# Background transform of k·v: spectra stored from the background's clock, the next channel tile begun at once, transposes seven or nine ticks behind the product

## The chip, the cores and the metric

The kernel runs on one core of one Trainium2 chip. The metric is the device time of one execution in microseconds, less is better. A time given for a kernel is the median of its runs; the profile comes from one more execution, which is read on its own time.

## The reference

Two rounds of a long-convolution layer and a feed-forward layer, each with a residual and a layer norm, on 2048 tokens of 1024 channels, in fp32:

```python
def _A_ref(q, k, v, shift_k, ssm_k, ssm_D):
    ...
    kv = k_shift * v                     # k_shift: causal depthwise conv over 4 tokens
    ...
    y_f = kv_f * kf_f                    # spectra over 2*S of kv and of ssm_k
    y = irfft(y_f)[:S]                   # so: a causal depthwise conv over all 2048 tokens
    y = y + kv * ssm_D
    return q * y

def _B_ref(x, w1, b1, w2, b2):
    h = relu(x @ w1 + b1) ** 2           # 1024 -> 3584
    return h @ w2 + b2                   # 3584 -> 1024

x = A_q
x = x + _A_ref(_layernorm(x), A_k, A_v, ...)
x = x + _B_ref(_layernorm(x), B_w1, ...)
x = x + _A_ref(_layernorm(x), A_k, A_v, ...)
x = x + _B_ref(_layernorm(x), B_w1, ...)
```

Of the convolution only q depends on the layer before. The convolution of k·v with `ssm_k` depends on the inputs alone, so one result serves both rounds.

## The kernel before

The tokens are cut into four blocks of 512 (`sb` or `b`, 0 to 3), the channels into eight tiles of 128 (`c`). The feed-forward matmuls run in seven **units**, each a layer and a token block, in the order (0,0), (1,0), (0,1), (0,2), (1,1), (0,3), (1,2), the last one together with (1,3). An fp32 product is made of three fp32r matmuls of a high and a low half (`mm3`, lines 353, 354 and 355), so nearly all of TensorE's work carries one of these three lines. A unit is a list of **steps** of twelve such matmuls. The weights for them are loaded (`wr`), cast to the high half on ScalarE (line 1102), and the low half is subtracted on VectorE, sometimes on GpSimd (line 1110). Line 1098 loads halves that an earlier unit stored in `wd_m`; line 1118 stores them. Line 1587 makes the low half of a feed-forward activation.

Beside the steps goes the **background**, which makes the convolution of blocks 1 to 3 while the units run. It consists of generators that are advanced by a *tick* at a time; what they issue in a tick stands between two pieces of the main work.

- `fwd_x` transforms one channel tile of k·v, `fwd_g` one of `ssm_k`. Each has its stream over blocks and channel tiles. `fwd_tick` advances both streams by one yield. It is called 1.4 times per step in the first three units and less often later, not at all in the last steps of most units, and once more wherever the product stream has nothing to do.
- `prod_stream` multiplies the stored spectra on GpSimd (line 543), sums on VectorE (line 547), folds on GpSimd or VectorE (lines 693 to 698), transforms back on TensorE (for block 1 line 613), and evicts on ScalarE (line 619) into a row buffer named `wr`, of the ring that also holds weights as they are loaded.

The background's clock `plag` (a `Later`) counts the ticks of the product stream; `plag.at(n, f, ...)` calls `f` n ticks on. When both streams are through with a tile, its entry in `fwd_done` is set three ticks on, and only then is its spectrum read (line 643).

`fwd_x` for one tile is: load k and v (lines 373 and 375), four ticks, scale on ScalarE (380), three multiply-adds on VectorE for the four-token convolution (383), the product with v (385), then a number of empty ticks (386), then one bank of the PSUM ring `pt` is taken and TensorE transposes the product into it (called in line 389, issued in line 438). ScalarE copies the result out (393), for blocks 2 and 3 split into two halves (397 on ScalarE, 399 on VectorE). Two banks are taken for the transform (409 for block 1, three matmuls each for the others), the butterfly runs on VectorE (420, 421, 425), and three spectra go to `XD` in DRAM (430). `fwd_g` has the same shape, with its own lines: transform (472), and on VectorE 482 to 502, of which 501 and 502 are butterflies on `pt` and on `fk`.

The ring `pt` has two banks, shared by the transposes, both transforms and the inverse. Line 613's matmuls and line 438's use it in turn. An engine executes its instructions in the order in which the program issued them. So a place in the tick order is a place in every engine's queue: what TensorE finds there has to be ready, or all the matmuls behind it stand still.

The lines that the change touches are 386 (the number of empty ticks) and 426 to 431 (the store).

Of the kernel before, what the change touches and what calls it, by code (L numbers as in the profile page):

```python
# [248 lines left out]
def tile_h3_mlp(ctx: ExitStack, tc: tile.TileContext, q, kT, vT, shk, ssmT, ssmD, w1, b1, w2, b2,  # L249
# [28 lines left out]
    def mkfx(shape, dt=F32):  # L278
        return cv.tile(shape, dt, name="fx", bufs=4)
# [68 lines left out]
    def give(*tiles):  # L348
        for o in tiles:
            held[slot.pop(id(o))[0]] = False  # L350

    def mm3(o, lh, ll, rh, rl, start, stop):
        PE.matmul(o, lh, rh, start=start, stop=False)  # L353
        PE.matmul(o, lh, rl, start=False, stop=False)  # L354
        PE.matmul(o, ll, rh, start=False, stop=stop)  # L355

    def hold(n):
        got = take(n)
        while not got:
            yield  # L360
            got = take(n)
        return got

    def dview(t, sb, c):
        return t[2 * c:2 * c + 2, :, BT * sb:BT * sb + BT].rearrange("g p b u -> p g b u")
# [5 lines left out]
    def fwd_x(sb, c):  # L371
        k4 = mkfx([P, T + 3])
        SY.dma_start(k4, kT[c * P:(c + 1) * P, sb * T:sb * T + T + 3])
        v4 = mkfx([P, T])
        SY.dma_start(v4, vT[c * P:(c + 1) * P, sb * T:(sb + 1) * T])
        for _ in range(FWD_WAIT):
            yield
        ks = mkfx([P, T])
        w = shkt[:, c]
        A.activation(ks, k4[:, 3:], AF.Copy, scale=w[:, 0:1])  # L380
        yield
        for s in range(1, 4):
            V.scalar_tensor_tensor(ks, k4[:, 3 - s:T + 3 - s], w[:, s:s + 1], ks, op0=OP.mult, op1=OP.add)
        yield
        V.tensor_mul(ks, ks, v4)
        for _ in range(4 if sb == 1 else 7):
            yield
        o, = yield from hold(1)
        transposes(o, ks)
        yield  # L390
        if sb <= PLAIN:
            xt = mkfx([P, T])
            A.copy(xt, o)
        else:
            hi = mkfx([P, T], F32R)
            lo = mkfx([P, T], F32R)
            A.copy(hi, o)
            yield
            V.tensor_sub(lo, o, hi.bitcast(F32))
        yield  # L400
        give(o)
        yield
        oa = yield from hold(2)
        for e in range(2):
            for r in range(2):
                q_ = slice(e * 256, e * 256 + 256)
                ou = oa[e][:, r * 256:r * 256 + 256]
                if sb <= PLAIN:
                    PE.matmul(ou, plain[0][:, 2 * e + r], xt[:, q_], start=True, stop=True)
                else:  # L410
                    mm3(ou, fh[:, 2 * e + r], fl[:, 2 * e + r], hi[:, q_], lo[:, q_], True, True)
        yield
        odd = mkfx([P, T])
        A.copy(odd, oa[1])
        yield
        xo = cv.tile([P, 2, T], F32, name="fy", bufs=1)
        xv = xo.rearrange("p r (n u c) -> p u (r n) c", u=2, c=CG)
        ev = oa[0].rearrange("p (n c) -> p n c", c=CG)
        ov = odd.rearrange("p (n c) -> p n c", c=CG)
        V.tensor_add(xv[:, 0], ev, ov)  # L420
        V.tensor_sub(xv[:, 1], ev, ov)
        yield
        give(*oa)
        x2 = mkfx([P, T])
        V.tensor_add(x2, xo[:, 0], xo[:, 1])
        yield
        yield
        for i in range(3):
            t = x2 if i == 2 else xo[:, i]
            SY.dma_start(dview(XD[i], sb, c), t.rearrange("p (g b u) -> p g b u", g=2, b=BT))  # L430
        yield

    def transposes(o, ks):
        ov = o.rearrange("p (e g b c) -> p e b g c", e=2, g=2, b=BT)
        kv = ks.rearrange("p (b t e) -> p e b t", b=BT, e=2)
        for e in range(2):
            for b in range(BT):
                PE.transpose(ov[:, e, b], kv[:, e, b], ident)
# [75 lines left out]
    plag, slag = Later(), Later()  # L514
# [3 lines left out]
    def fwd_stream(kind, fwd):  # L518
        for sb in range(1, NB):
            if sb > PLAIN:  # L520
                const_split()
            for c in range(KT):
                yield from fwd(sb, c)
                half_done[kind].add((sb, c))
                if all((sb, c) in d for d in half_done.values()):
                    plag.at(3, fwd_done.add, (sb, c))

    streams = [fwd_stream("x", fwd_x), fwd_stream("g", fwd_g)]

    def fwd_tick():  # L530
# [1613 lines left out]
    for s, (k, u, c, a, i, tts, w) in enumerate(steps):  # L2144
# [38 lines left out]
        if k == "m1":  # L2183
# [9 lines left out]
            for kk in range(4):  # L2193
                t = slice(kk * P, (kk + 1) * P)
# [8 lines left out]
        elif k == "w2":  # L2203
# [7 lines left out]
            for n in range(2):  # L2211
                t = slice(n * P, (n + 1) * P)
# [11 lines left out]
        else:  # L2224
# [5 lines left out]
            for tt in tts:  # L2230
                t = slice(tt * P, (tt + 1) * P)
# [124 lines left out]
```

## Time and profile before

| | before |
|---|---|
| median of 3 runs | 2680.07 us (2679.81 to 2684.74) |
| profiled execution, its own time | 2686.72 us |
| its span | 2684.9 us |
| TensorE (PE) busy | 2623.7 us, 98% of the span |
| VectorE (DVE) busy | 2009.8 us, 75% |
| ScalarE (ACT) busy | 1108.6 us, 41% |
| GpSimd (POOL) busy | 1027.9 us, 38% |
| DMA queue, share of 16 engines | 83.3% |

The span is the time from the first to the last instruction in the trace; 1.8 us of the execution's own time lie around it. The profile names an engine, a line and an operation with the tile written and the tile read (`out<-in`), and where an engine stood idle it names the instruction that released it. PEclk is the granted TensorE clock as a share of full speed: 1.00 is 2.4 GHz, 0.50 is 1.2 GHz.

### The profile page before, as it was taken

The numbers are of one execution on the slowest core, as the hardware profiler recorded it, in microseconds if no ns is written. First come the engines' busy times: TensorE is split into PE (matmuls) and PEld (weight loads), VectorE is DVE, ScalarE is ACT, GpSimd is POOL, SyncE is SP. The second block draws the span as 40 slices with busy tenths as digits, with TensorE's granted clock in tenths as the row PEclk, the third lists the DMA queues.
The fourth block names the chain that finished last, engine by engine and source line by source line (L and its number), as shares of the span: only waits on it lengthen the run. The fifth ranks groups of instructions, "written<-read, shape, count | busy, mean of one in ns | idle before, by whom it ended". The sixth has DMA issues, their size and how long they took to land.

```text
span 2684.9 us, 36134 instructions
## 1 busy us (share of the span) xinstructions
PE 2623.7 (98%) x12388; PEld 2197.9 (82%) x12388; DVE 2009.8 (75%) x2948; ACT 1108.6 (41%) x1891; POOL 1027.9 (38%) x651
## 2 busy tenths in 40 slices
PE   7999999899999999999999999999999999999999
PEld 6888787787888888888888888888788778888887
DVE  7879888789887877779677765456777788877553
ACT  4454344443444333343232422345444565454342
POOL 2436665256551744427554275000100207535111
PEclk9999999999999999999999999999999999999999
DMA  8789898689989999888987888689889787888663
GB/s 254 262 300 313 293 305 280 231 292 357 345 296 315 308 329 304 273 300 303 340 303 255 306 293 306 207 260 321 304 296 304 269 323 251 263 247 317 230 194 121
DMA packets 380264, 763.16 MB, mean 284 GB/s; under 512 B 44064, under 2 KB 159408, under 8 KB 377008
## 3 DMA queue, kind: packets, MB, share of 16 engines
q1 hardware_dynamic: 380080, 760.85, 83.3%
q8 instruction: 98, 1.61, 0.2%
q14 instruction: 86, 0.70, 0.1%
HBM read 583.49 MB, written 177.21 MB: 283 GB/s over the span
## 4 chain that ended last, share of the span: by engine, by line
PE 79%; DVE 8%; DMA 8%; issue 2%; ACT 2%; POOL 2%; SPq 1%; DVEq 0%; ACTq 0%; POOLq 0%
PE p L353 22%; PE p L354 22%; PE p L355 22%; PE pt L354 2%; PE pt L353 2%; PE pt L355 2%; DMA wr<-w 2%; PE p L1184 2%; DMA whl<-wd_m 2%; DMA cg<-gd 1%; DVE whl L1110 1%; POOL cp L543 1%; DVE sm L547 1%; DVE st L714 0%; DMA cx<-xd 0%
## 5 line engine op out<-in xcount | busy, mean ns | idle before, releaser
L543 POOL TENSOR_TENSOR cp<-cx,cg 128x384 f32<-128x384 f32 (+5 forms) x288 | 544.6, 1904 | 567.7 <-DVE sm L547 378.2
L353 PE MATMUL p<-xh,whl 128*128 128x512 f32 (+1 forms) x1504 | 579.1, 385 | 10.6 <-ACT wr L1924 5.7
L355 PE MATMUL p<-xh,whl 128*128 128x512 f32 (+1 forms) x1504 | 574.9, 382 | 3.5 <-DVE whl L1110 3.0
L354 PE MATMUL p<-xl,whl 128*128 128x512 f32 (+1 forms) x1504 | 574.6, 382 | 0.1
L1110 DVE TENSOR_TENSOR whl<-wr,whl 128x512 fp32r<-128x512 f32 x486 | 430.1, 896 | 130.9 <-ACT whl L1102 126.0
L1102 ACT CAST whl<-wr 128x512 fp32r<-128x512 f32 x546 | 332.4, 619 | 468.7 <-PE p L355 291.7
L353 PE MATMUL p<-whl,rh 128*128 128x512 f32 x1204 | 475.9, 395 | 7.1 <-DMA whl<-wd_m 5.7
L354 PE MATMUL p<-whl,rh 128*128 128x512 f32 x1204 | 471.1, 391 | 2.6 <-POOL whl L1110 1.7
L355 PE MATMUL p<-whl,rl 128*128 128x512 f32 x1204 | 470.6, 391 | 0.0
L353 PEld LDWEIGHTS p<-xh,whl 128*128 128x128 f32 x1504 | 284.9, 189 | 66.2 <-ACT wr L1924 6.4
L355 PEld LDWEIGHTS p<-xh,whl 128*128 128x128 f32 x1504 | 284.7, 189 | 59.1 <-DVE whl L1110 3.4
L354 PEld LDWEIGHTS p<-xl,whl 128*128 128x128 f32 x1504 | 284.7, 189 | 52.4 <-DVE xl L1497 0.3
L1587 DVE TENSOR_TENSOR rl<-wr,rh 128x512 fp32r<-128x512 f32 x140 | 141.7, 1012 | 178.7 <-ACT rh L1584 178.6
L353 PEld LDWEIGHTS p<-whl,rh 128*128 128x128 f32 x1204 | 227.3, 189 | 55.9 <-DMA whl<-wd_m 4.8
L1110 POOL TENSOR_TENSOR whl<-wr,whl 128x512 fp32r<-128x512 f32 x60 | 87.5, 1461 | 483.9 <-ACT whl L1102 426.4
L354 PEld LDWEIGHTS p<-whl,rh 128*128 128x128 f32 x1204 | 227.2, 189 | 49.8 <-DVE whl L1110 2.5
L355 PEld LDWEIGHTS p<-whl,rl 128*128 128x128 f32 x1204 | 226.9, 188 | 47.8
L547 DVE TENSOR_REDUCE sm<-cp 128x128 f32<-128x384 f32 (+5 forms) x288 | 249.4, 874 | 10.2 <-POOL cp L543 10.2
L1579 ACT ACTIVATE wr<-p,b1t 128x512 f32<-128x512 f32 x138 | 95.3, 690 | 369.8 <-PE p L355 368.9
L1707 DVE TENSOR_TENSOR acc<-p,acc 128x512 f32<-128x512 f32 x152 | 99.8, 686 | 83.6 <-PE p L355 83.6
L693 POOL TENSOR_TENSOR sm<-sm 128x512 f32<-128x512 f32 x48 | 69.1, 1440 | 136.2 <-DVE sm L547 130.3
L355 PE MATMUL p<-whl,tq 128*128 128x512 f32 x276 | 107.4, 389 | 0.0
(376 smaller groups left out, 4264.0 us busy)
## 6 DMA issues: line engine op xcount, KB each, us to landing
whl<-wd_m SPq DMA_DIRECT2D x318, 512.0 KB, 5.5
wr<-w SPq DMA_DIRECT2D x442, 256.0 KB, 5.5
wd_m<-whl SPq DMA_DIRECT2D x70, 512.0 KB, 6.3
wr<-td SPq DMA_DIRECT2D x112, 256.0 KB, 5.1
cx<-xd SPq DMA_DIRECT2D x48, 512.0 KB, 5.8
cg<-gd SPq DMA_DIRECT2D x48, 512.0 KB, 6.8
tq<-hd SPq DMA_DIRECT2D x24, 1024.0 KB, 7.2
gd<-fg SPq DMA_DIRECT2D x72, 256.0 KB, 6.4
```

The source lines that it names most:

```text
L353: PE.matmul(o, lh, rh, start=start, stop=False)
L354: PE.matmul(o, lh, rl, start=False, stop=False)
L355: PE.matmul(o, ll, rh, start=False, stop=stop)
L543: G.tensor_mul(pr.rearrange("p c i -> p i c"), xt[:, 0:j + 1], gt[:, j::-1])
L547: V.tensor_reduce(sm[:, ty, jj], st["pr"], axis=AX.X, op=OP.add)
L693: E.tensor_add(s[:, 1:3], s[:, 1:3], s[:, 0:1].to_broadcast([P, 2, s.shape[2]]))
L1102: A.copy(t[:, 0], raws[n]["t"])
L1110: ENG[e[n % len(e)]].tensor_sub(t[:, 1], raws[n]["t"], t[:, 0].bitcast(F32))
L1184: PE.matmul(o, lh, r, start=start, stop=stop)
L1579: A.activation(r, st["o"], AF.Relu, bias=b1t[:, st["f"]:st["f"] + 1])
L1587: V.tensor_sub(st["lo"], st["r"]["t"], st["hi"].bitcast(F32))
L1707: V.tensor_add(accs[tt][:, d], o, accs[tt][:, d])
```

## The change

```diff
@@ fwd_x
         V.tensor_mul(ks, ks, v4)
-        for _ in range(4 if sb == 1 else 7):
+        for _ in range(7 if sb == 1 else 9):
             yield
         o, = yield from hold(1)
         transposes(o, ks)
...
         x2 = mkfx([P, T])
         V.tensor_add(x2, xo[:, 0], xo[:, 1])
+        plag.at(2, store_x, sb, c, [xo[:, 0], xo[:, 1], x2])
         yield
-        yield
-        for i in range(3):
-            t = x2 if i == 2 else xo[:, i]
+
+    def store_x(sb, c, ts):
+        for i, t in enumerate(ts):
             SY.dma_start(dview(XD[i], sb, c), t.rearrange("p (g b u) -> p g b u", g=2, b=BT))
-        yield
```

Three things change. Between the product and its transposes there are seven empty ticks in place of four for block 1, and nine in place of seven for blocks 2 and 3. The three stores are issued two ticks of `plag` after the last addition, by the clock and no longer inside the stream. And the stream gives up two of the three yields around the stores, so that the next tile's loads are issued in the tick after the last addition. A tile of block 1 takes one tick more than before (three added, two dropped), a tile of blocks 2 and 3 as many as before.

Three places show how the instructions move. The first is **TensorE** near the middle of the first unit, at the fifth channel tile of block 1 (tiles counted from the first one that goes through `fwd_x`). `p_...` are the main work's PSUM tiles, `whl` the weights, `rh` and `rl` the activations, `ident,fx` the transposes, `sm,yh` the inverse. Before:

```order
 L354 MATMUL p_2898<-whl,rh 128x512
 L355 MATMUL p_2898<-whl,rl 128x512
 L613 MATMUL pt<-sm,yh 128x128 x4
 L438 MATMUL pt<-ident,fx 128x2x64 x4
 L353 MATMUL p_2895<-whl,rh 128x512
 L354 MATMUL p_2895<-whl,rh 128x512
```

and with the change, where `L613 MATMUL pt<-sm,yh 128x128 x8` stands twelve rows above the transposes:

```order
 L354 MATMUL p_2889<-whl,rh 128x512
 L353 MATMUL p_2890<-whl,rh 128x512
 L354 MATMUL p_2890<-whl,rh 128x512
 L355 MATMUL p_2890<-whl,rl 128x512
 L438 MATMUL pt<-ident,fx 128x2x64 x4
 L353 MATMUL p_2887<-whl,rh 128x512
```

The transposes move down: in the built programs 16 main matmuls lie between the tile's product (line 385 on VectorE) and its transposes before, and 44 now. For the nine tiles from the first on the count goes from 76, 24, 24, 28, 16, 44, 28, 16, 44 to 76, 36, 40, 44, 44, 40, 56, 28, 556.

The second place is **VectorE** at the same tile. Before:

```order
 L501 TENSOR_TENSOR fg<-pt,fg 128x2x2x64
 L502 TENSOR_TENSOR fg<-pt,fg 128x2x2x64
 L383 SCALAR_TENSOR_TENSOR fx<-fx,shkt 128x512 x3
 L501 TENSOR_TENSOR fg<-fk 128x2x2x64
 L502 TENSOR_TENSOR fg<-fk 128x2x2x64
 L1110 TENSOR_TENSOR whl<-wr,whl 128x512
 L385 TENSOR_TENSOR fx<-fx 128x512
 L1110 TENSOR_TENSOR whl<-wr,whl 128x512
 L1587 TENSOR_TENSOR rl<-wr,rh 128x512
 L1110 TENSOR_TENSOR whl<-wr,whl 128x512
```

and with the change:

```order
 L383 SCALAR_TENSOR_TENSOR fx<-fx,shkt 128x512 x3
 L501 TENSOR_TENSOR fg<-pt,fg 128x2x2x64
 L502 TENSOR_TENSOR fg<-pt,fg 128x2x2x64
 L1110 TENSOR_TENSOR whl<-wr,whl 128x512
 L385 TENSOR_TENSOR fx<-fx 128x512
 L501 TENSOR_TENSOR fg<-fk 128x2x2x64
 L502 TENSOR_TENSOR fg<-fk 128x2x2x64
 L1110 TENSOR_TENSOR whl<-wr,whl 128x512
 L1587 TENSOR_TENSOR rl<-wr,rh 128x512
 L1110 TENSOR_TENSOR whl<-wr,whl 128x512 x2
```

The product keeps its neighbours; only a pair of `fwd_g`'s butterflies moves from ahead of it to behind it.

The third place is **SyncE's DMA queue** in the first unit, at the first tile that is stored from the background (the change against the kernel before):

```order
-L430 DMA xd_74<-fy 128x2x256
-L430 DMA xd_75<-fy 128x2x256
-L430 DMA xd_76<-fx 128x2x256
 L373 DMA fx<-kT 128x515
 L375 DMA fx<-vT 128x512
 L1092 DMA wr<-w 128x512 x2
-L1118 DMA wd_m_0_0_2_1739<-whl 128x1024
+L1118 DMA wd_m_0_0_2_1736<-whl 128x1024
+L431 DMA xd_74<-fy 128x2x256
+L431 DMA xd_75<-fy 128x2x256
+L431 DMA xd_76<-fx 128x2x256
```

The stores move behind the next tile's loads of k and v and behind three more transfers of weights.

## Rows read from the trace of the kernel before

**Rows 1.** The page: busy time of each engine, and VectorE's share in 40 slices.

```profile
PE 2623.7 (98%) x12388; PEld 2197.9 (82%) x12388; DVE 2009.8 (75%) x2948; ACT 1108.6 (41%) x1891; POOL 1027.9 (38%) x651
...
DVE  7879888789887877779677765456777788877553
```

**Rows 2.** TensorE's waits, whole span: total us, times, longest us.

```profile
PE pt L438 <- DVE fx L385: 7.6, 3, 5.0
...
PE pt L613 <- DVE fg L502: 2.1, 1, 2.1
...
PE pt L354 <- DVE yl L579: 0.7, 1, 0.7
```

**Rows 3.** TensorE's instructions at the fifth tile: start us, us, engine, line.

```profile
294.31 0.39 PE L354 MATMUL p<-whl,rh 128*128 128x512 f32 x1
294.54 0.39 PE L355 MATMUL p<-whl,rl 128*128 128x512 f32 x1
294.77 1.05 PE L613 MATMUL pt<-sm,yh 128*128 128x128 f32 x8
300.78 1.09 PE L438 MATMUL pt<-ident,fx 128*128 128x128 f32 x4 [4.96 <-DVE fx L385]
```

**Rows 4.** TensorE's instructions at the fourth tile, same columns.

```profile
257.72 1.05 PE L613 MATMUL pt<-sm,yh 128*128 128x128 f32 x8
260.94 0.72 PE L438 MATMUL pt<-ident,fx 128*128 128x128 f32 x4 [2.17 <-DVE fx L385]
```

**Rows 5.** Stretches: us, busy us of each engine, PEclk, DMA share, GB/s.

```profile
261.80:265.20 3.40, 3.40 (x10) 2.63 (x9) 3.40 (x7) 3.34 (x7) 0.00 (x0) 0.50 1.02 338
...
299.40:306.20 6.80, 5.42 (x15) 4.47 (x16) 6.49 (x12) 1.49 (x3) 3.31 (x4) 0.50 1.01 303
...
446.10:449.60 3.50, 3.50 (x11) 2.82 (x11) 3.46 (x6) 0.38 (x1) 2.36 (x2) 0.51 0.00 0
...
637.30:640.70 3.40, 3.40 (x9) 2.64 (x8) 3.40 (x6) 0.18 (x1) 0.49 (x1) 0.50 1.04 378
```

**Rows 6.** VectorE's instructions at the fifth tile: start us, us, engine, line.

```profile
291.73 0.42 DVE L501 TENSOR_TENSOR fg<-pt,fg 128x256 f32<-128x256 f32 x1
...
292.39 3.69 DVE L383 SCALAR_TENSOR_TENSOR fx<-fx,shkt 128x512 f32<-128x512 f32 x3
296.00 1.22 DVE L501 TENSOR_TENSOR fg<-fk 128x256 f32<-128x256 f32 x1
297.14 1.49 DVE L502 TENSOR_TENSOR fg<-fk 128x256 f32<-128x256 f32 x1
298.56 1.48 DVE L1110 TENSOR_TENSOR whl<-wr,whl 128x512 fp32r<-128x512 f32 x1
299.95 0.68 DVE L385 TENSOR_TENSOR fx<-fx 128x512 f32<-128x512 f32 x1
...
301.76 0.68 DVE L1110 TENSOR_TENSOR whl<-wr,whl 128x512 fp32r<-128x512 f32 x1
```

**Rows 7.** GpSimd's instructions at the same time.

```profile
295.49 4.00 POOL L543 TENSOR_TENSOR cp<-cx,cg 128x384 f32<-128x384 f32 x3
```

**Rows 8.** VectorE at the fourth tile; the 1.88 us are three instructions.

```profile
260.12 0.68 DVE L385 TENSOR_TENSOR fx<-fx 128x512 f32<-128x512 f32 x1
...
261.93 1.88 DVE L1110 TENSOR_TENSOR whl<-wr,whl 128x512 fp32r<-128x512 f32 x3
```

**Rows 9.** Line 383, all instances: ns min/median/max, first and last start.

```profile
L383 DVE SCALAR_TENSOR_TENSOR fx<-fx,shkt x72: 706/753/2793, 147.3 to 1411.8; 128x512 f32<-128x512 f32 x72
```

**Rows 10.** Line 619, all instances, and what it waited for (us, times).

```profile
L619 ACT ACTIVATE wr<-pt x16: 377/384/389, 228.7 to 574.1; 128x256 f32<-128x256 f32 x16
...
  DVE whl L1110: 12.1, 4
```

**Rows 11.** SyncE's queue: what the spectrum stores waited for.

```profile
SPq L430 <- DVE fx L425: 12.4, 10, 3.5
```

**Rows 12.** TensorE's waits from 500 to 650 us, columns as in rows 2.

```profile
PE p L353 <- DMA whl<-wd_m: 2.9, 2, 2.1
```

## The prediction

> **What bounds the kernel.** The page comes first: TensorE is busy 98% of the span, VectorE 75%, and in the first third of the span 80 to 90% [rows 1]. A change in the background's order adds no matmul and takes none away, so it can only act on the 2% in which TensorE stands, and on the time that it runs at half clock. Second, the list of TensorE's waits: of those that the edited lines can reach there are three on line 385, 7.6 us together, and one of 2.1 us on line 502 [rows 2]. Third, TensorE's instructions in time: two of the three waits are at the fourth tile, 2.17 us [rows 4], and at the fifth, 4.96 us [rows 3]; the third is what is left of 7.6, 0.5 us. Fourth, the clock: about each long wait there is a stretch with a granted clock of 0.50, and after it the clock is 1.00 again [rows 5]. So a wait costs its idle time and then half of the busy time in its slow stretch.
>
> VectorE tells why TensorE waits at the fifth tile. The product (line 385) is issued 16 matmuls ahead of the transposes, 16 x 0.23 = 3.7 us at the spacing of two starts [rows 3], but VectorE reaches it 8.6 us after that place (3.7 and the 4.96 that TensorE waits): it is late. Its three multiply-adds take 3.69 us where three at the shortest take 2.1 [rows 6, 9], line 501 takes 1.22 us where it took 0.42 a moment before, line 502 takes 1.49 and line 1110 1.48 against 0.68 in the same rows [rows 6]. With 0.42 for line 502 too, the excess is 1.6 + 0.8 + 1.1 + 0.8 = 4.3 us. From 295.49 to 299.49 GpSimd runs three multiplications [rows 7], and from 299.95 VectorE's operations have their short times again.
>
> **The change, part by part.** The sum is made against the profiled execution, 2686.72 us. The median of the runs is 6.65 us lower, and the difference is carried over to it.
>
> *Three more ticks ahead of the transposes, block 1.* The distances count main matmuls between product and transposes.
> - Fourth tile: 28 become 44. TensorE reaches the new place 16 x 0.23 = 3.6 us after the old one, at 258.77 + 3.6 = 262.4; the product was through at 260.8 [rows 8]. The wait goes: 2.17 us, and half of 3.40 busy us at half clock, 1.70 [rows 5]; 3.87 in all. But the transposes now stand directly behind two inverses, and a bank of the ring comes free only when line 619 has evicted it into a row of the weight ring, which waits for line 1110 to have read the row (line 619 waited for line 1110 four times, 12.1 us) [rows 10]. Line 1110 is through at about 262.6 (the first of the three in 1.88 us from 261.93) [rows 8], and two evictions are 2 x 0.38 [rows 10], so 263.3 against 262.4: I take 1.0 us for this new wait. Its ends are 0 (TensorE met the same neighbours before without a wait) and 2.2, the old wait. Net -2.9.
> - Fifth tile: 16 become 44. TensorE arrives at 295.82 + 28 x 0.23 = 302.2, the product was through at 300.6 [rows 6]. The wait goes with 4.96 us and half of 5.42 busy us, 2.71 [rows 3, 5]; 7.67 in all. The same eviction stands in front: line 1110 is through at 302.4 [rows 6], with 2 x 0.38 us that is 1.0 us after TensorE. Ends 0 and 5.0, the old wait. Net -6.7.
> - The third wait, 0.5, goes to nothing: its tile gets 28 more matmuls, 6.4 us. Net -0.5.
> - The end of the first unit: line 613 waited 2.06 us for line 502, with 1.75 us for the half of 3.50 busy us at half clock [rows 2, 5], 3.8 in all. This inverse stays 24 matmuls behind its VectorE work, and only the order of the operations about it changes. Ends 0 and 3.8; I take the middle. Net -1.9.
>
> *New short distances.* Moving the whole stream against the rest puts other pairs close together. One transform of ssm_k (line 472) now stands 2 matmuls behind the butterfly that frees its bank, and at two tiles of block 2 the second matmul of the transform (line 354) stands 1 behind line 399, which makes its operand; 13 was the least before. The nearest row is a wait of line 354 for a low half from VectorE, 0.7 us [rows 2]. I take it for each: +2.1. From below they cost nothing, where VectorE is in step; from above VectorE's lag at the fifth tile, 8.6 less one matmul, 8.4 each.
>
> *Two ticks more for blocks 2 and 3.* No wait of TensorE on line 385 is left from there on, so nothing is gained. The ninth tile's transposes go from the end of the first unit into the second (556 matmuls); what follows them is background that nobody waits for in that unit. 0, and if that cover went the price would be one more wait of the kind above, 0.7.
>
> *The store.* It issues the same three transfers, some ticks later by the clock, behind the next tile's loads and three transfers of weights. SyncE waited for VectorE in front of them, 12.4 us at line 425 alone [rows 11], and all loads behind them waited along. That goes, or shrinks. Nobody on TensorE waits for these spectra: their first reader stands at least a tick behind, on the same clock. 0; for a gain see the first rival.
>
> Sum: -2.9 - 6.7 - 0.5 - 1.9 + 2.1 = **-9.9 us**: 2676.8 us for a profiled execution, **2670.2** for the median. What TensorE is late for next are the loads of stored weights near 630 us. With every wait at its better end it is -(3.87 + 7.67 + 0.5 + 3.8) = -15.8, 2664.2.
>
> **The rule that speaks against it.** The longer VectorE operations stand beside GpSimd's multiplications [rows 6, 7]. The Trainium skill says why, on the page "SBUF — State Buffer", section "Who interferes with whom": VectorE's two-input operations and GpSimd's accesses to SBUF lock a shared pair of ports against each other, and whoever has it holds the other off completely. The trace agrees so far as 1.22 and 1.49 us beside GpSimd stand against 0.42 a moment before [rows 6]. By that rule more ticks leave VectorE's delay as it is and only move the place where TensorE meets it; by it the change ends like the second rival below, by the trace alone like the sum above.
>
> **The rivals.**
> 1. *More than the sum.* Earlier loads on SyncE also end the waits for stored weights: 2.9 us from 500 to 650 us [rows 12], with 1.7 for the half clock behind them [rows 5]. For it: the spectrum stores no longer hold the queue up [rows 11]. Against it: the DMA share in the slow stretch there is 1.04 [rows 5], the transfers have no room. Time: 2670.2 - 4.6 = 2665.6. Chance 0.12.
> 2. *The wait moves.* VectorE's delay returns at the fifth tile, and the eviction in front of the transposes takes it over. 4.3 us of excess on top of the new 1.0 is 5.3, more than the 4.96 removed, and with the slow clock behind it nothing is gained: -9.9 + 7.0 = -2.9, 2677.2. If the end of the first unit keeps its wait too, +1.9, 2679.1. For it: eviction and transposes both hang on VectorE's queue [rows 6, 10]. Against it: the order there puts two more operations behind the product and none ahead. It decides as soon as VectorE is 4 us late at the new place. Time 2679. Chance 0.30.
> 3. *Slower.* At the two places in block 2 where line 354 stands 1 matmul behind line 399, VectorE is as late as at the fifth tile: 8.4 us each and 2.7 for the clock behind each, 22.2 in place of the 1.4 counted, so -9.9 - 1.4 + 22.2 = +10.9, 2691.0. For it: the matmul stands directly behind its operand in the order. Against it: those places are near 555 and 690 us, where VectorE has a fifth of the time free [rows 1]. It is slower by more than 0.2% once each of the waits is above 5.6 us. Chance 0.10.
>
> That the change does not do what it says is answered by the built order: the distances grow as counted, but for one tile, where 44 become 40.
>
> **How the numbers follow.** 0.2% (5.4 us) is about what a measurement of this kernel can tell from no change, so faster means under 2674.7. The forecast has 0.48, and with the first rival faster has 0.60. The second rival is within 0.2%: 0.30. The third is 0.10. The forecast's own bounds are 2664 to 2675. The range takes in the first rival with all better ends (2680.1 - 15.8 - 4.6 = 2660) and the second, and goes half way into the third: 2660 to 2686.
>
> **What would show it.** Right: no wait of line 438 on line 385 from 250 to 450 us, PEclk 1.00 at the fourth and fifth tiles, waits of 1 us or less in front of the transposes, and TensorE's end of the first unit some 10 us earlier in the profile. Wrong: a wait of line 438 or 613 on line 619 or on VectorE of more than 4 us in the first unit (second rival), waits of line 354 on line 399 over 5 us in block 2 (third), or a slow stretch in a place that has none now. If the first unit gains its 10 us and the end does not, the loads near 630 us took them back.

## The result: slower by 0.4%, with the waits moved and none saved

| | before | the change |
|---|---|---|
| median | 2684.01 us (8 runs, 2678.66 to 2689.23) | 2693.95 us (8 runs) |
| ratio, 95% interval | 1 | 1.0041 [1.003, 1.0051] |
| profiled execution | 2686.72 us, span 2684.9 | 2692.31 us, span 2690.5 |

The change is **slower** by 0.41%; the forecast was faster by 0.37%, and 2693.95 us lies above its range. (One of the eight runs took 5359 us, twice the others; the rest lie between 2689.88 and 2699.88 with a median of 2693.19, and the ratio is made without it.) The two profiled executions differ by 5.6 us, the medians by 9.9; what follows accounts for the 5.6.

The head of the page, to be held against [rows 1], shows no engine with more work of its own:

```profile
span 2690.5 us, 36163 instructions
## 1 busy us (share of the span) xinstructions
PE 2625.0 (98%) x12388; PEld 2198.9 (82%) x12388; DVE 2008.3 (75%) x2948; ACT 1107.0 (41%) x1891; POOL 1025.1 (38%) x651
```

TensorE's waits over the whole span (total us, times, longest) answer to [rows 2]:

```profile
PE p L355 <- DVE whl L1110: 11.7, 5, 4.8
PE p L353 <- DMA whl<-wd_m: 6.8, 7, 1.9
...
PE pt L354 <- DVE fx L399: 2.0, 1, 2.0
...
PE pt L353 <- DVE fy L421: 1.8, 1, 1.8
...
PE pt L438 <- DVE fx L385: 0.3, 1, 0.3
```

The waits on the product (line 385), 7.6 us before, are down to 0.3. In their place the main matmuls of line 355 wait for the low half of their weights (line 1110), 11.7 us against 3.0. From 250 to 450 us, where the forecast had nearly all of its gain, the list of the kernel before has only the first two lines of [rows 2], on lines 385 and 502. With the change it is:

```profile
PE p L355 <- DVE whl L1110: 7.3, 2, 4.8
PE pt L613 <- POOL sm L697: 1.8, 1, 1.8
PE pt L613 <- POOL sm L698: 0.4, 1, 0.4
PE pt L438 <- DVE fx L385: 0.3, 1, 0.3
```

The sums are 9.7 and 9.8 us: other instructions wait, for as long. That the sums are so nearly equal is no rule: the shifted and spread versions below have 3.4 to 11.6 us from 200 to 450 us. The longest new wait is at the fourth tile and begins 3.0 us earlier than the old one there [rows 4], at 255.78 against 258.77 us. TensorE's instructions there with the change (start us, us):

```profile
255.16 0.39 PE L353 MATMUL p<-xh,whl 128*128 128x512 f32 x1
255.39 0.39 PE L354 MATMUL p<-xl,whl 128*128 128x512 f32 x1
260.56 0.79 PE L355 MATMUL p<-xh,whl 128*128 128x512 f32 x1 [4.79 <-DVE whl L1110]
```

VectorE's instructions say why. First the kernel before, then the change, at the same tile:

```profile
253.37 0.75 DVE L1587 TENSOR_TENSOR rl<-wr,rh 128x512 fp32r<-128x512 f32 x1
254.04 1.22 DVE L1110 TENSOR_TENSOR whl<-wr,whl 128x512 fp32r<-128x512 f32 x1
255.19 4.34 DVE L383 SCALAR_TENSOR_TENSOR fx<-fx,shkt 128x512 f32<-128x512 f32 x3
```

```profile
253.91 3.51 DVE L383 SCALAR_TENSOR_TENSOR fx<-fx,shkt 128x512 f32<-128x512 f32 x3
257.34 0.41 DVE L501 TENSOR_TENSOR fg<-pt,fg 128x256 f32<-128x256 f32 x1
257.68 0.41 DVE L502 TENSOR_TENSOR fg<-pt,fg 128x256 f32<-128x256 f32 x1
258.01 0.82 DVE L1587 TENSOR_TENSOR rl<-wr,rh 128x512 fp32r<-128x512 f32 x1
258.75 1.76 DVE L1110 TENSOR_TENSOR whl<-wr,whl 128x512 fp32r<-128x512 f32 x1
```

Before, the step's weights (line 1110) were done at 255.3, and the three multiply-adds came behind them. With the change the multiply-adds stand ahead of them in VectorE's queue, and the weights are done at 260.5.

At the sixth tile TensorE waits 2.55 us, but not for that reason: 66 operations of line 1110 on weights and 15 of line 1587 stand ahead of its multiply-adds, as before. VectorE's lines before and with the change, and TensorE's:

```profile
332.10 2.31 DVE L383 SCALAR_TENSOR_TENSOR fx<-fx,shkt 128x512 f32<-128x512 f32 x3
```

```profile
333.08 3.69 DVE L383 SCALAR_TENSOR_TENSOR fx<-fx,shkt 128x512 f32<-128x512 f32 x3
...
338.12 1.51 DVE L501 TENSOR_TENSOR fg<-fk 128x256 f32<-128x256 f32 x1
...
342.02 0.79 PE L355 MATMUL p<-xh,whl 128*128 128x512 f32 x1 [2.55 <-DVE whl L1110]
```

The multiply-adds now run beside GpSimd's folds and butterflies and take 3.69 us in place of 2.31; line 501 on `fk` takes 1.51 beside a multiplication in place of 0.42; and a pair of `fwd_g`'s butterflies on `pt` (0.8 us) has come behind the multiply-adds.

The clock follows the longer waits (stretch, busy us, PEclk), to be held against [rows 5]:

```profile
259.70:266.50 6.80, 5.94 (x18) 4.97 (x19) 5.91 (x9) 4.01 (x7) 1.68 (x2) 0.50 1.03 371
341.60:345.00 3.40, 2.98 (x7) 2.40 (x8) 3.40 (x7) 2.88 (x6) 0.08 (x1) 0.50 0.70 236
437.20:440.60 3.40, 3.40 (x10) 2.92 (x11) 3.40 (x3) 2.16 (x5) 3.40 (x3) 0.50 0.39 115
299.40:306.20 6.80, 6.80 (x40) 5.94 (x40) 6.80 (x11) 1.24 (x3) 2.57 (x2) 1.00 0.68 228
```

The fifth tile is as forecast (last row: clock 1.00, no wait), but there is a slow stretch of 6.8 us at the fourth now, and a new one at the sixth.

The rest of the loss stands behind the first unit. Of the matmuls that read a weight, counted in order, the 1301st (near 464 us, at the start of the second unit) comes 2.0 us later than before, the 2001st (617 us) 7.0, the 2251st (686 us) 1.9, the 2501st (749 us) 6.2 and the last 5.7. Between the second and the third of these places the kernel before loses time on stored weights [rows 12] that the change does not. The steps up hold the two new waits of the transforms in block 2, on lines 421 and 399. Ahead of both, VectorE had stood idle until GpSimd had made a product of spectra (line 543) that line 547 was to sum; what stands behind line 547 in VectorE's queue is late by that. Lines of VectorE and TensorE with the change:

```profile
601.27 0.82 DVE L547 TENSOR_REDUCE sm<-cp 128x128 f32<-128x640 f32 x1 [2.86 <-POOL cp L543]
...
604.54 0.68 DVE L421 TENSOR_TENSOR fy<-pt,fx 128x512 f32<-128x512 f32 x1
605.27 0.39 PE L353 MATMUL pt<-fg,fh 128*128 128x256 f32 x1 [1.84 <-DVE fy L421]
...
694.89 0.95 DVE L547 TENSOR_REDUCE sm<-cp 128x128 f32<-128x768 f32 x1 [2.46 <-POOL cp L543]
697.16 0.39 PE L354 MATMUL pt<-fx,fh 128*128 128x256 f32 x1 [1.97 <-DVE fx L399]
```

and this idle time over the whole span, before and with the change:

```profile
DVE sm L547 <- POOL cp L543: 10.2, 15, 1.7
```

```profile
DVE sm L547 <- POOL cp L543: 44.5, 26, 4.1
```

From 455 to 760 us it is 0 before and 13.6 us with the change. GpSimd itself had stood idle 8.45 and 7.19 us until spectra had been loaded, before the multiplications from 599.65 and 689.38 us.

### The profile page after: what moved, and what is told of

Read it like the earlier page. It is cut to its first block, busy times and chain, and to the rows that moved or that the text cites. A ratio compares the mean times of both kernels' runs of the same rounds, so it can differ in the third digit from the quotient of the medians.

```text
span 2690.5 us, 36163 instructions
## 1 busy us (share of the span) xinstructions
PE 2625.0 (98%) x12388; PEld 2198.9 (82%) x12388; DVE 2008.3 (75%) x2948; ACT 1107.0 (41%) x1891; POOL 1025.1 (38%) x651
## 4 chain that ended last, share of the span: by engine, by line
PE 75%; DVE 9%; DMA 8%; issue 3%; ACT 2%; POOL 1%; SPq 1%; DVEq 0%; ACTq 0%; POOLq 0%
PE p L355 22%; PE p L354 22%; PE p L353 22%; PE pt L354 2%; PE pt L355 2%; PE pt L353 2%; DMA wr<-w 2%; PE p L1184 1%; DMA cg<-gd 1%; DVE whl L1110 1%; DMA wd_m<-whl 1%; DVE sm L547 1%; DMA whl<-wd_m 1%; DMA fx<-kT 0%; POOL cp L543 0%
## 5 line engine op out<-in xcount | busy, mean ns | idle before, releaser
L355 PE MATMUL p<-xh,whl 128*128 128x512 f32 (+1 forms) x1504 | 576.6, 383 | 13.1 <-DVE whl L1110 11.7
L355 PEld LDWEIGHTS p<-xh,whl 128*128 128x128 f32 x1504 | 285.3, 190 | 69.8 <-DVE whl L1110 13.6
L547 DVE TENSOR_REDUCE sm<-cp 128x128 f32<-128x384 f32 (+5 forms) x288 | 250.0, 875 | 45.8 <-POOL cp L543 44.5
```

Source lines behind the costliest of these rows:

```text
L547: V.tensor_reduce(sm[:, ty, jj], st["pr"], axis=AX.X, op=OP.add)
```

## The experiments

In the expectations "theory A" to "theory G" are the explanations in the order in which they were formed. By *late* is meant that VectorE finishes an operation after TensorE has passed the place in the order where it was issued. Ratios are to the kernel before, with 95% intervals. Lines of the variants can stand some places further down; they are named by their number in the kernel before.

### Which part of the change does it?

**Ticks alone.** Line 386 as in the change, the store and its yields as before.

> Only the empty ticks are changed (seven and nine); the store stays inside the stream with its three yields, so a tile of block 1 is three ticks longer than before. Theory A (VectorE's delay is kept): at each channel tile VectorE falls 8 to 11 us behind the place where its work was issued; more ticks take the waits of line 438 on line 385 away (7.6 us before), and TensorE then meets the same delay at the next weights (line 1110), 4 us or more in the first unit: time within 0.3% of before or slower. Theory B (phase): the waits on line 1110 of the change come from one tick more per tile, which shifts the x stream against the g stream; three ticks more shift it three times as fast, so waits on line 1110 or another of VectorE's operands, at other tiles than in the change, 0 to 15 us in all. Theory C (the store's late place does the harm): without it the gain of the forecast shows, 0.2 to 0.5% faster than before.

Measured: 2712.61 us, 1.0116 [1.0102, 1.013], the slowest of all. Yet its first unit is much better than before: from 200 to 450 us TensorE's only waits over half a microsecond are 2.1 us on line 421, 1.5 on line 1110 and 0.8 on line 1707, and the 1201st matmul that reads a weight starts 10.7 us earlier than in the kernel before. So theory A was wrong in its strict form: VectorE's delay need not be met. In this order line 1110 stood directly ahead of the multiply-adds at the fourth, fifth and seventh tiles, and at the fifth they took 2.32 us in place of 3.69. Theory B's waits at other places came, but the loss is twice its 15 us at most; C's gain did not come. The stream, though, comes 24 ticks late to the end of the unit, where the program issues what is left of the block in one go, and there the loss starts. Up to 512 us the 10.7 us ahead have become 1.7, and 27 us more are lost later:

```profile
451.14 0.39 PE L353 MATMUL p<-whl,rh 128*128 128x512 f32 x1
457.63 0.79 PE L354 MATMUL p<-whl,rh 128*128 128x512 f32 x1 [6.10 <-DVE whl L1110]
```

**Store and yields alone.**

```diff
-        for _ in range(7 if sb == 1 else 9):
+        for _ in range(4 if sb == 1 else 7):
```

(an edit of the change, so the store stays late and the two yields stay out)

> Only the store and the yields around it are changed (ticks four and seven), so every tile is two ticks shorter than before. Theory A: transposes close behind the product meet VectorE's delay, waits of line 438 on line 385 of 5 us or more in the first unit as before, time within 0.3% of before. Theory B: two ticks less per tile shift the streams against each other the other way; waits appear on line 1110 as in the change, 0.2 to 0.5% slower. Theory C: as slow as the whole change, 0.4%.

Measured: 2695.16 us, 1.0046 [1.0033, 1.0058]. The wait on line 385 fell to 0.8 us although the ticks were the old ones, and waits on lines 1110 (3.9), 1707 (2.3), 697 (1.8) and 502 (1.5) took its place. Theory A is out for this run; B and C both fit it.

**Tiles as long as before.** The change with `6 if sb == 1 else 9`.

> The whole change, but six ticks for block 1 in place of seven, so that every tile takes as many ticks as before and the x stream does not drift against the g stream. Theory A: VectorE's delay of 8 to 11 us is still met, at line 1110 or at an eviction in front of the transposes, 3 us or more in the first unit: within 0.3% of before. Theory B: no wait of 2 us or more on line 1110 before 500 us, those on line 385 gone too: 0.2 to 0.5% faster than before. Theory C: 0.4% slower.

Measured: 2697.07 us, 1.0057 [1.0045, 1.007], with 4.6 and 4.1 us of waits on line 1110 in the first unit. Theory B is out in this form: the extra tick per tile is not what does it. Theory A's waits are there, but the time is above its 0.3%.

**The store late, nothing else.** The call of `plag.at` in place of the three stores, all three yields kept.

> The store is issued by the clock, two ticks behind the last addition, but all yields and the ticks four and seven stay, so nothing else moves. Theories A and B: within 0.15% of before, with the waits of line 438 on line 385 as before, 5 to 8 us in all. Theory C: 0.2 to 0.4% slower, with waits on transfers.

Measured: 2684.34 us, 1.0009 [1.0, 1.0018], with 7.6 us of waits on line 385 as before. Theory C is out; the store's place costs 0.09%, 0.18% (4.8 us) at most.

So each of these shifts of the stream, by more ticks or by fewer, cost 0.4 to 1.2%, and which operand was late differed each time. That asks what makes VectorE late at all.

### Less work for VectorE

**The change and the kernel before, lighter.** In both:

```diff
-        for s in range(1, 4):
+        for s in range(1, 2):
```

> The change, with two of the three multiply-adds of line 383 left out (k is convolved over two tokens in place of four), which takes 2 x 0.7 to 1.2 us of VectorE's work out of each tile and moves nothing else. Theory D (the change puts line 383 ahead of the weights' low half of the same step, line 1110, so TensorE meets VectorE's delay there): the waits of line 355 on line 1110 of 4.8 us near 256 us and 2.6 us near 340 us fall to under 2 us each, and the time is 5 to 14 us below the change's 2694. Rival E (the wait is the weights' own: their load, their cast on ScalarE or a buffer, and line 383 only stands beside it): both waits stay within 1 us of what they were, time within 0.15% of the change.

> The kernel before, with the same two multiply-adds left out. Theory D: the same delay of VectorE is what line 438 waits for on line 385 (2.2, 5.0 and 0.5 us), so these waits fall to under 3 us together, time 5 to 12 us below before; and with the work gone the kernel before and the change differ by less than their 0.4%. Rival E: the waits on line 385 fall as well, but the change stays 0.4% slower than the kernel before, both without the two operations.

Measured: the lighter change 2674.97 us, 0.9978 [0.9966, 0.9989]; the lighter kernel before 2673.64 us, 0.9968 [0.9957, 0.998]. The two operations are worth 8.1 us to the kernel before, run beside it, and 17 us (by the two ratios) to 19 (by two medians taken at different times) to the change, more than the 5 to 14 expected. Without them the two differ by 1.3 us, with intervals that overlap. In the lighter change the fourth tile's wait is 0.91 in place of 4.79 us; in the lighter kernel before the fifth tile's is what is left, 3.96 us where under 3 was expected:

```profile
260.29 0.50 PE L354 MATMUL p<-whl,rh 128*128 128x512 f32 x1 [0.91 <-DVE whl L1110]
```

```profile
295.52 1.10 PE L438 MATMUL pt<-ident,fx 128*128 128x128 f32 x4 [3.96 <-DVE fx L385]
```

Rival E is out: the weights' wait in the first unit is VectorE's lateness.

**Seven ticks for block 1 too, the rest as before.**

> The kernel before with seven ticks for block 1 as well; blocks 2 and 3 keep seven, the store stays in the stream. A tile of block 1 is three ticks longer, as in the run with the ticks alone, which was 10.7 us ahead of before at the end of the first unit and lost 9 us between 424 and 503 us and 25 more later. Theory D: the first unit gains the same 9 to 11 us. If the loss between 424 and 503 us comes from the later position of the stream, it stays (time 2684 to 2695); if it came from blocks 2 and 3 with nine ticks, it goes, and the time is 5 to 10 us below before.

Measured: 2706.94 us, 1.0093 [1.0076, 1.011]. The first unit gains again (the wait on line 385 is gone), and from 440 to 500 us the list of waits has line 1110 with 7.4 us, where before it was 0.7. So the loss at the unit's end is there without the nine ticks of blocks 2 and 3, and goes with the stream's late arrival; the times expected were too low by 12 us, since blocks 2 and 3 lose as well.

### The order of the multiply-adds

**The change, spread.** A yield after each multiply-add, ticks five and seven.

> The change, with the three multiply-adds of line 383 in three ticks in place of one and two empty ticks less (five and seven), so a tile is as long as in the change. Theory D: weights' low halves (line 1110) now pass between them, so no wait of 2 us or more on line 1110 before 450 us, and the time is 3 to 10 us below the change's 2694. Rival (what counts is VectorE's work in the tile, not its order): waits move but their sum before 450 us stays within 2 us of the change's 11, time within 0.15% of the change.

Measured: 2687.32 us, 1.0018 [1.0008, 1.0027], 6.6 us below the change (6.2 by the two ratios). Waits before 450 us are 5.0 us in all, 1.5 of them on line 1110, as theory D expected: the order counts too, with VectorE's work unchanged. Here the eviction that the prediction priced at 1.0 us turned up once:

```profile
PE pt L438 <- ACT wr L619: 1.8, 1, 1.8
```

**The kernel before, spread; spread and earlier.** The loads are issued ahead of the last addition of the tile before, and the four ticks behind them become two (first run) or one (second run, which has five and eight ticks at line 386):

```diff
         give(*oa)
+        load_kv(*next_tile)
...
-        for _ in range(FWD_WAIT):
+        for _ in range(2):
...
         for s in range(1, 4):
             V.scalar_tensor_tensor(ks, ...)
-        yield
+            yield
```

> The kernel before, with the three multiply-adds of line 383 in three ticks (the third, fourth and fifth of the tile) in place of one; for this the loads of k and v are issued three ticks earlier, ahead of the last addition of the tile before. Product, transposes, transform and store keep their ticks, and a tile its length. Theory D (the harm is three multiply-adds in one piece ahead of an operand that TensorE needs soon): waits on line 385 and on line 1110 before 450 us under 5 us together (9.7 before, all waits there), time 3 to 8 us below before. Rival (only the position of the whole tile against the weights counts, and any move leads off a place that was found by trial): slower than before by 5 us or more.

> As the run before, but the multiply-adds stand in the second, third and fourth tick and the product in the fifth, five ticks ahead of the transposes, which stay where they were. Theory D: no wait of 1 us or more on line 385, time 3 to 10 us below before. Rival: slower than before by 5 us or more.

Measured: 2683.63 us, 1.0007 [0.9998, 1.0016], and 2681.89 us, 1.0004 [0.9995, 1.0013]. Neither gains 3 us, nor loses the rival's 5. In the first the wait at the fifth tile is 6.2 us; in the second it is gone, and 2.8 us on line 1707, 2.9 on line 502 and 1.9 on line 619 stand for it.

**Product earlier, transposes in place.** As above without the yields between; product three ticks earlier (seven ahead of the transposes), then one.

> The kernel before with scale, multiply-adds and product three ticks earlier and the transposes where they were: seven ticks between product and transposes as in the change, a tile as long as before, the store as before. Theory D: the waits on line 385 go, but at the fourth tile the line 1110 of the step now stands behind line 383 as in the change, and TensorE waits there 2 us or more; time from before to 0.4% slower. If instead the longer tile of the change does the harm: 5 to 10 us below before.

> The same with one tick in place of three: scale, multiply-adds and product one tick earlier, five ticks ahead of the transposes (eight for blocks 2 and 3). In its order line 1110 of the step stands behind line 383 at the fourth tile again. Theory D: as the run before, a wait of 2 us or more on line 1110 near 257 us, time within 0.4% of before or slower. Rival as there: 3 to 8 us below before.

Measured: 2687.35 us, 1.002 [1.0011, 1.0029] with this wait at the fourth tile, as expected:

```profile
PE p L355 <- DVE whl L1121: 5.9, 2, 4.7
```

and 2687.69 us, 1.002 [1.0011, 1.0029] with 1.8 us there (2 or more was expected) and the fifth tile's wait on the product back, 4.7 us. Line 1121 is line 1110 of this variant.

### Its own work, or time lost beside GpSimd?

**Work moved to GpSimd.** Line 425 with `G` for `V` (first run); also the third butterfly pair, lines 501 and 502 on `fk` (the other three, on the kernel before, the change, and the spread and earlier variant).

> The kernel before, with the last addition of fwd_x (line 425, 0.7 to 1.3 us of VectorE's time per tile) on GpSimd; nothing else moves. Theory D (VectorE's own work makes the delay): the waits of line 438 on line 385 fall by 1 to 2 us each, time 2 to 5 us below before. Rival F (what VectorE saves it loses again beside GpSimd, whose queue grows by about the same): within 0.15% of before, or slower.

> As the run before, and one of the three butterfly pairs of fwd_g as well (lines 501 and 502 on fk, 0.8 us per tile alone, up to 2.7 us beside GpSimd). Theory D: VectorE has 1.5 to 4 us less per tile, as much as in the lighter kernel (two multiply-adds less: 8 us below before), time 4 to 8 us below before. Rival F: within 0.15% of before, or slower.

> The change, with the same addition and butterfly pair on GpSimd. Theory D: the waits on line 1110 near 256 and 340 us (4.8 and 2.6 us) fall under 2 us each, time 8 to 15 us below the change's 2694, so at or below the kernel before. Rival F: within 0.2% of the change.

> The variant with multiply-adds spread and early (2682, equal to before), with the same addition and butterfly pair on GpSimd. Theory D: 4 to 9 us below before, the fastest of all that compute the reference. Rival F: within 0.15% of before or slower.

Measured: 1.0057 [1.0044, 1.007], 1.0061 [1.0047, 1.0074], 1.0064 [1.0051, 1.0076] and 1.0052 [1.0039, 1.0064]; 2694.71, 2697.12, 2697.25 and 2694.59 us. None gains, against theory D: the first, second and fourth are 0.5 to 0.6% slower than what they were made from, the third is 0.1 to 0.2% above the change, too little to tell. Rival F has the direction but not the reason: in the first, VectorE is busy 27.2 us less (1982.6 us), so it does not lose again in work what it was spared. But GpSimd is busy 28.7 us more (1056.6), VectorE's idle time in front of line 547 goes from 10.2 to 27.1 us, and the wait on the product has grown from 7.6 to 13.4 us:

```profile
PE pt L438 <- DVE fx L385: 13.4, 5, 6.5
```

```profile
299.95 1.21 DVE L501 TENSOR_TENSOR fg<-fk 128x256 f32<-128x256 f32 x1
301.09 1.49 DVE L502 TENSOR_TENSOR fg<-fk 128x256 f32<-128x256 f32 x1
302.50 1.48 DVE L1110 TENSOR_TENSOR whl<-wr,whl 128x512 fp32r<-128x512 f32 x1
```

The second fence is VectorE at the fifth tile of that run: the long operations are as long as in [rows 6], to 0.01 us. What it was spared lay elsewhere. The idle time fits a GpSimd that is later with its products and holds VectorE up; no run shows that apart.

**Half the multiplications.** GpSimd multiplies only half of the channels; VectorE sums that half twice:

```diff
-            G.tensor_mul(pr.rearrange("p c i -> p i c"), xt[:, 0:j + 1], gt[:, j::-1])
+            G.tensor_mul(pr[:, 0:64].rearrange("p c i -> p i c"), xt[:, 0:j + 1, 0:64], gt[:, j::-1, 0:64])
...
-            V.tensor_reduce(sm[:, ty, jj], st["pr"], axis=AX.X, op=OP.add)
+            for e in range(2):
+                V.tensor_reduce(sm[:, ty, jj, 64 * e:64 * e + 64], st["pr"][:, 0:64], axis=AX.X, op=OP.add)
```

> The kernel before, with GpSimd multiplying only half of the channels of each product of spectra (line 543); VectorE sums that half twice, so its own work stays about the same. Theory G (VectorE is late by the time it loses beside GpSimd): the operations of 1.2 to 1.5 us at the fifth tile fall towards 0.4 to 0.7, the waits from 250 to 450 us fall from 9.7 us to under 5, time 5 to 12 us below before. Theory D alone (VectorE's own amount of work): those waits stay within 2 us of 9.7, time within 0.15% of before.

> The change, with the same halving. Theory G: the waits on line 1110 near 256 and 340 us (7.3 us together) fall under 3, time 10 to 18 us below the change, so equal to the kernel before with the same halving within 0.2%. Theory D alone: the waits from 250 to 450 us stay within 2 us of 9.8, and the change stays 0.4% slower than the other.

Measured: kernel before 2668.29 us, 0.9957 [0.9943, 0.997]; change 2668.15 us, 0.9958 [0.9945, 0.997]. The halving takes 12.6 us from the kernel before, run beside it, and 22 (by the two ratios) to 26 (by medians taken at different times) from the change, for both more than theory G expected, and the two are equal. The waits from 250 to 450 us are 3.8 us in the first (3.6 of them at the fifth tile, on line 385) and 1.7 in the second. At the fifth tile of the first, lines 501, 502 and 1110 fell only to 0.81, 0.94 and 1.07 us, not to the 0.4 to 0.7 expected, and the multiply-adds still take 3.69. The granted clock was 1.00 from 250 to 450 us in both, so the wait of 3.6 us brought no slow stretch. The costliest groups of VectorE's work, before and then halved (busy us, mean ns of one):

```profile
L1110 DVE TENSOR_TENSOR whl<-wr,whl 128x512 fp32r<-128x512 f32 x486 | 430.1, 896 | 130.9 <-ACT whl L1102 126.0 <-DMA yd<-wr 4.4
L547 DVE TENSOR_REDUCE sm<-cp 128x128 f32<-128x384 f32 (+5 forms) x288 | 249.4, 874 | 10.2 <-POOL cp L543 10.2
L1707 DVE TENSOR_TENSOR acc<-p,acc 128x512 f32<-128x512 f32 x152 | 99.8, 686 | 83.6 <-PE p L355 83.6
L383 DVE SCALAR_TENSOR_TENSOR fx<-fx,shkt 128x512 f32<-128x512 f32 x72 | 84.3, 1171 | 2.2 <-ACT fx L380 0.4
```

```profile
L1111 DVE TENSOR_TENSOR whl<-wr,whl 128x512 fp32r<-128x512 f32 x486 | 381.8, 796 | 136.1 <-ACT whl L1103 133.3 <-DMA fk<-kd 1.7 <-issue 0.2
L548 DVE TENSOR_REDUCE sm<-cp 128x64 f32<-128x192 f32 (+5 forms) x576 | 266.1, 507 | 4.0 <-POOL cp L543 3.9
L1708 DVE TENSOR_TENSOR acc<-p,acc 128x512 f32<-128x512 f32 x152 | 101.0, 688 | 96.5 <-PE p L355 96.5
L383 DVE SCALAR_TENSOR_TENSOR fx<-fx,shkt 128x512 f32<-128x512 f32 x72 | 69.9, 971 | 3.7 <-ACT fx L380 1.8
```

The sums cost VectorE 16.7 us more, as the edit has it, but the same 486 weight operations take 100 ns less each and the same 72 multiply-adds 200 ns less. Line 1707, one of whose inputs is in PSUM, does not change (686 and 688 ns). The trace of the kernel before shows the loss directly, when each operation is set against GpSimd's instructions by their times. Of the 486 weight operations 337 ran with no GpSimd instruction beside them and took 672 to 695 ns, 685 on average; 149 ran beside one and took 1373 ns on average, 2914 at most. Line 501 on `fk`, in SBUF, takes 418 ns alone and 983 beside GpSimd (14 and 10 operations); on `pt`, in PSUM, it takes 410 beside GpSimd (28), and line 1707 takes 686 either way (33 beside). So what VectorE loses beside GpSimd is real, and the waits of the first unit go with it. One thing is not told apart: the halving also lets the sums start earlier (the idle time in front of line 547 falls from 10.2 to 3.9 us, in the change from 44.5 to 23.5), and how much of the 12.6 us that is stays open.

That the change and the kernel before are equal in both pairs does not mean that every place is. From the 251st weight matmul to the 1301st the change is 2.4 us slower than the kernel before as they are, 2.6 us faster with half the multiplications and 4.5 us faster with two multiply-adds less. From there to the last one it is slower each time: 3.7, 3.9 and 6.4 us. So with VectorE less late the change does gain in the first unit, and what it loses behind it stays. These are single profiled executions.

## Why the prediction was wrong

**The step that failed is the fourth tile's, "The wait goes: 2.17 us", and with it the first part's gain.** It treated the wait as belonging to the pair of product and transposes, to be cured by distance. VectorE reached the product 28 x 0.23 + 2.17 = 8.6 us behind its place. With the wait on the product gone, the next operand that was needed from VectorE's queue was met late, and that was line 1110. The prediction looked at line 1110 only where it stood behind the product, done at 262.6 [rows 8], and only as what the eviction waits for; the weights of the step before, done at 255.3 ahead of the multiply-adds, it did not look at. It compared VectorE's order at one tile, the fifth, where the weights do keep their place, and took that for all: at the fourth, one operation each of lines 1587 and 1110 now stands behind the multiply-adds. And it took VectorE's times as fixed. At the sixth tile, for which it has no term, the order of the weights is the same, but other operations stand beside GpSimd, and they take longer.

The first unit's terms, by idle time and half of the busy time at half clock:
- Fourth tile, forecast -2.9: 4.79 + 2.97 in place of 2.17 + 1.70, so +3.9.
- Fifth tile, forecast -6.7: gone altogether, -7.7, and the eviction cost nothing there. The mechanism held.
- Third wait (the seventh tile's), forecast -0.5: gone there, and 0.3 has come at the eighth, -0.2.
- End of the unit, forecast -1.9: 1.79 + 0.42 and 1.70 for the clock in place of 2.06 + 1.75, so 0.1. It waits now for GpSimd's butterfly (lines 697 and 698).
- Sixth tile, not forecast: 2.55 + 1.49, +4.0.

The sum is +0.1 us where -12.0 was forecast. Of the signs that the prediction set, none names line 1110; "a slow stretch in a place that has none now" came true at the sixth tile.

**The short distances** were a right guess of the wrong size: lines 399 and 421 cost 2.0 and 1.8 us where 0.7 was taken for each of three places; no slow clock followed, and of the upper bound of 8.4 us nothing was seen. The third rival was thus right in direction and in one of its places (697 us), though not in its price. What made VectorE late there is a path at which the prediction put nothing, from the loaded spectra by GpSimd and line 547 to all that stands behind in VectorE's queue. "Nobody on TensorE waits for these spectra" is true only of direct waits.

**The first rival** happened, but did not decide: the waits for stored weights from 500 to 650 us, 2.9 us [rows 12], are gone from the list, and from 617 to 686 us the change makes up 5.1 us where the rival had 4.6. In the run with ticks alone, whose store is the old one, they are gone too, so the store is not shown to be the reason. **The second rival** had the mechanism, a delay of VectorE that returns and is taken over, but at the wrong heir: it named the eviction, and its 2679 us left no room for more than the old wait. The store alone was rightly costed at nothing (0.18% at most).

**The rule that spoke against the change was right about the loss, and it had no size.** In the prediction it was weighed and left with 0.30. Its reading of line 501 (1.22 us against 0.42) compares the form on `fk` with the form on `pt`; the numbers by form, above, bear it out. The Trainium skill's page "SBUF — State Buffer", section "Who interferes with whom", gives a reason: a VectorE instruction with two inputs in SBUF contends with a GpSimd instruction that reads SBUF, over a shared pair of ports. The trace agrees: 1373 against 685 ns for line 1110, and 686 either way for line 1707, which has an input in PSUM. That more ticks only move the delay does not follow from it: with ticks alone the first unit was 10.7 us faster, since other operations came to stand beside GpSimd.

What is shown: the change moves waits in the first unit; take away load on VectorE, in either way, and the waits on line 1110 there go but for 0.9 and 0.3 us, the forecast's gain in that unit appears in part, and the change and the kernel before take equal time. What is shown by traces alone: behind the first unit TensorE waits at lines 421 and 399, with VectorE idle for GpSimd ahead of both. From 455 to 760 us this idle time is 7.7 to 25.1 us in the nine versions that move the transposes or take yields from the store, and 0 to 3.8 in the eleven others, the kernel before among them. No run takes away that idle time alone, and why the spectra come late to GpSimd in these versions stays open. No version found here beats the kernel before with the whole computation done.

## What to carry to other kernels

Before a wait on an engine that is late is moved, write down how late the engine is, place by place, and ask for each of its next results how far behind its reader stands. Less work, or less time lost beside another engine, takes lateness away; moving instructions may do so in one place and make it in another. A tick more or less in an interleaved stream moves all its instructions against the main work, so the order of the late engine has to be compared at every place where it is late, not at the worst one, and so has what runs on the engine that slows it down. Look also for the late engine's own idle time. When work is to be moved to an idle engine, check first whether the two slow each other down.

## What the runs showed that was not expected

- One addition per tile moved from VectorE to GpSimd (24 operations of 1.16 us on average, 27.8 us in all, that take 1.5 us there) made the kernel 0.57% slower, though VectorE was busy 27.2 us less.
- Three ticks more per tile in block 1 and two in the others cost 31 us (2681.52 to 2712.61), with a first unit that was 10.7 us faster. VectorE's idle time for GpSimd's products was 70.4 us there, against 10.2.
